# Token weights fetched and placed earlier, two squares moved from ScalarE to GpSimd, and one value cast moved later, in a fused attention and mixer kernel

## The chip, the cores and the metric

The kernel runs on one core of one Trainium2 chip. A core has a matrix engine (TensorE, PE in the profile; PEld is its loading of weights), VectorE (DVE), ScalarE (ACT), GpSimd (POOL), and SyncE (SP), which here only issues transfers. Each engine executes its own instructions in order; semaphores tie them together. The metric is the device time of one execution in microseconds (us); less is better. Three executions of the kernel before took 393.38, 394.13 and 394.23 us, median 394.13.

## What is computed

Cosine attention for 8 batches of 12 heads, sequence 448, head size 64, and behind it an MLP mixer over the tokens and then the channels:

```python
# q, k, v: (8, 12, 448, 64) fp32, tau = 0.1
q_n = q / (norm(q, axis=-1) + 1e-6)
k_n = k / (norm(k, axis=-1) + 1e-6)
scores = q_n @ k_n^T / tau
attn = softmax(scores)                        # exp and division by the row's sum
x = (attn @ v), heads side by side            # (8, 448, 768)
h = relu(x^T @ w_tok1) @ w_tok2               # (448, 256), (256, 448): over tokens
u = x + h^T
h2 = relu(u @ w_ch1) @ w_ch2                  # (768, 1536), (1536, 768): over channels
out = u + h2                                  # fp32
```

## The kernel before

The work goes by pairs of heads: 48 pairs, six per batch; three pairs make a "half" of a batch, the unit in which q, k and v are loaded. Of the 448 rows of a head, 384 lie as three rows on each of 128 partitions (the main part, tiles `qm`, `km`, `vm`); the last 64 are loaded apart (`xq`, `xk`, `xv`).

A pair goes through these steps:

- **Norms.** `squares` (L182) squares q and k of the pair into a tile `sq`, of which two exist; `squares_x` (L187) does the last 64 rows of a half's three pairs into one tile `sqx`. `square` (L176) runs on the engine that it is given; its instruction is L178 on ACT, L180 elsewhere. `sums` (L191) and `sums_x` (L196) add up per head and row on DVE (L193, L197), and `rnorms` (L199) makes inverse norms by four activations on ACT (L201 to L204).
- **Scaling.** `scaled` (L206) and `scaled_x` (L214) multiply k and q by the inverse norms into `kq` (L211, L217, L222), on POOL but for pair 0.
- **Transposes.** For the first 15 pairs, `tpose` (L253) turns `kq` around on PE (L243, L247, L248) into a PSUM tile, and `qk_copy` (L260) brings it to SBUF on DVE (L261).
- **Scores.** `score` (L295) multiplies k by q for a third of the main rows (PE, L301; two matmuls beside each other) and takes the exponential on ACT (L302); `score_x` (L305) does the last rows (L308, L309).
- **Values.** `cast_v` (L165) and `cast_vx` (L169) turn v of a half into fp16 (L166, on DVE for halves 0 to 2; L172, on POOL). `pv` (L311) multiplies by the exponentials (PE, L320, L322); a column of ones in the values gives the sums, and DVE takes reciprocals (L326) and multiplies (L327) to make `x`.
- **Token mixing.** `m_tok1` (L337) multiplies by `w1t` (L341) and DVE applies the relu into `r` (L344). `m_tok2` (L348) multiplies by `w2t` (L361), adds `x` by a matmul with the identity (L366) and DVE copies the result into `ut` (L368).
- **Channel mixing.** When a batch's six pairs are through, its units `m_ch1` (L389, relu on ACT at L391) and `m_ch2` (L404, DVE adds at L407, SP sends) go into a queue, and `feed` (L438) takes some from it in every slot.

PSUM has two small tiles (tag "b": transposes, U, the channel products) and three large ones (tag "s": scores, values, psR), so a product waits until the consumer of an earlier one has emptied its tile.

The order is written out by hand: everything under `tc.manual_schedule()` (L512) is issued in the program's order on each engine. First comes a prologue for pair 0 (L513 to L592); then a loop over `i`, here called slots (L593). Slot `i` computes the scores of pair `i`, the values of pair `i - 1`, and in the first slots the token mixing of earlier pairs. Tables say in which slot what is begun: `sq_at` for squares, `sum_at` for their sums, `rn_at` for inverse norms, `sc_at` for scaling, `cast_at` and `castx_at` for the casts, and so on (L455 to L481).

The token weights have a path of their own. `weights_tok` (L140) issues three transfers from POOL: the main rows of `w_tok1`, its last 64 rows, and `w_tok2` into a staging tile `w2n`. They are issued at the end of the prologue (L589). `place_w2` (L146) copies `w2n` in the order that the kernel's rows have into `w2t` on DVE: the main part (L147) and the last 64 columns behind it (L149); `place_w2_odd` (L151) writes the same 64 columns in front, for batches with an odd number (L152). `place_w2` comes at the end of slot 2, `place_w2_odd` at the end of slot 3. Pair 0's U needs `w2t` in slot 3.

In slot 0 the squares of pair 3 begin half 1: q and k of the pair, then xq and xk, all four on ACT. The cast of half 1's values is issued in slot 3 (`cast_at`), before the slot's U; pair 3's values are multiplied in slot 4.

SP issues the loads of q, k, v in the order of the prologue (L513 to L533), among them v of half 0 (L528), the rest of q and k of half 1 (L530, L531) and v of half 1 (L532); the loads for half 2 start in slot 0.

Of the kernel before, what the change touches and what calls it, by code (L numbers as in the profile page):

```python
# [16 lines left out]
def _bcast_free(ap: bass.AP, n: int) -> bass.AP:  # L17
    new_ap = list(ap.ap) + [[0, n]]
    return bass.AP(tensor=ap.tensor, offset=ap.offset, ap=new_ap)
# [3 lines left out]
def kernel(  # L23
# [12 lines left out]
    nc = tc.nc  # L36

    B, H, S, E = q.shape
# [5 lines left out]
    NC = 3  # L44
    SM = P * NC
    XR = S - SM
# [7 lines left out]
    NP_ALL = B * NPAIR  # L54
    HP = 3
    NHALF = 2 * B
# [19 lines left out]
    w1t = cst.tile([P, NC + 1, T], FP16, name="w1t")  # L76
    w2t = cst.tile([P, TT, XR + S], FP16, name="w2t")
# [12 lines left out]
    w2n = []  # L90
# [43 lines left out]
    def xh(at, n, w):  # L134
        return at[n // 2][:, w * (n % 2):w * (n % 2) + w]

    def mh(at, p):
        return at[p // HP][:, 2 * (p % HP):2 * (p % HP) + 2]

    def weights_tok():  # L140
        nc.gpsimd.dma_start(out=w1t[:, 0:NC, :], in_=moe_w_tok1[0:SM].rearrange("(p c) t -> p c t", c=NC))
        nc.gpsimd.dma_start(out=w1t[0:XR, NC, :], in_=moe_w_tok1[SM:S])
        w2n.append(mix.tile([P, TT, S], FP16, name="w2n", tag="gt16", bufs=1))
        nc.gpsimd.dma_start(out=w2n[0][:], in_=moe_w_tok2.rearrange("(tt p) s -> p tt s", p=P))

    def place_w2():  # L146
        nc.vector.tensor_copy(out=w2t[:, :, XR:S].rearrange("t a (c p) -> t a c p", c=NC),  # L147
                              in_=w2n[0][:, :, 0:SM].rearrange("t a (p c) -> t a c p", c=NC))
        nc.vector.tensor_copy(out=w2t[:, :, S:S + XR], in_=w2n[0][:, :, SM:S])  # L149

    def place_w2_odd():  # L151
        nc.vector.tensor_copy(out=w2t[:, :, 0:XR], in_=w2n[0][:, :, SM:S])  # L152

    def weights_ch1(i):
        n = C // 2
# [9 lines left out]
    def cast_v(n):  # L165
        (nc.vector if n < 3 else nc.gpsimd).tensor_copy(out=vts[n % NV][:, :, :, 0:E].rearrange("p g c e -> p (g c) e"),  # L166
                              in_=vm[n][:].rearrange("p g c e -> p (g c) e"))

    def cast_vx(n):  # L169
        for g in range(2):  # L170
            r = slice(XR * g, XR * (g + 1))
            nc.gpsimd.tensor_copy(out=vxs[n % NV][r, :, E1 * g:E1 * g + E], in_=xh(xv, n, HP)[r])  # L172
# [3 lines left out]
    def square(eng, out, src):  # L176
        if eng is nc.scalar:
            nc.scalar.activation(out=out, in_=src, func=AF.Square)  # L178
        else:
            eng.tensor_tensor(out=out, in0=src, in1=src, op=ALU.mult)  # L180

    def squares(p, eq, ek):  # L182
        sq[p] = nrm.tile([P, 2, 2 * NC, E], FP32, name=f"sq_{p}", tag="sq")
        for a, (eng, src) in enumerate(((eq, mh(qm, p)), (ek, mh(km, p)))):
            square(eng, sq[p][:, a], src.rearrange("p g c e -> p (g c) e"))

    def squares_x(n, eq, ek):  # L187
        square(eq, sqx[0:XR, 0:6], xh(xq, n, 6))
        square(ek, sqx[:, 6:9], xh(xk, n, HP))

    def sums(p, a0=0, a1=2):  # L191
        lo = 9 + 12 * (p % HP)
        nc.vector.tensor_reduce(out=ssqs[p // HP % 3][:, lo + 6 * a0:lo + 6 * a1],  # L193
                                in_=sq[p][:, a0:a1].rearrange("p a g e -> p (a g) e"), axis=AXX.X, op=ALU.add)

    def sums_x(n):  # L196
        nc.vector.tensor_reduce(out=ssqs[n % 3][:, 0:9], in_=sqx[:], axis=AXX.X, op=ALU.add)  # L197

    def rnorms(n, c0=0, c1=45):  # L199
        ssq, rn = ssqs[n % 3][:, c0:c1], rns[n % 3][:, c0:c1]  # L200
        nc.scalar.activation(out=rn, in_=ssq, func=AF.Ln, bias=tiny[:])  # L201
        nc.scalar.activation(out=rn, in_=rn, func=AF.Exp, scale=0.5)
        nc.scalar.activation(out=rn, in_=rn, func=AF.Ln, bias=eps[:])  # L203
        nc.scalar.activation(out=rn, in_=rn, func=AF.Exp, scale=-1.0)  # L204

    def scaled(p, eng):  # L206
        n, j = p // HP, p % HP
        for a, src in enumerate((mh(km, p), mh(qm, p))):
            lo = 9 + 12 * j + 6 * (1 - a)
            rn = rns[n % 3][:, lo:lo + 6].rearrange("p (g c) -> p g c", g=2)  # L210
            eng.tensor_tensor(out=kqs[n % 2][:, j, a, 0:NC, :].rearrange("p c (g e) -> p g c e", g=2),  # L211
                              in0=src, in1=_bcast_free(rn, E), op=ALU.mult)
# [28 lines left out]
    def tpose_main(p, pst, a):  # L241
        for c in range(NC):
            nc.tensor.transpose(pst[:, P * (4 * a + c):P * (4 * a + c + 1)], kqs[p // HP % 2][:, p % HP, a, c], id16[:])  # L243
# [61 lines left out]
    def score_x(p):  # L305
        qk, pt = qks[p], pts[p % 2]
        psX = ps2.tile([P, 2, 512], FP32, name=f"psX_{p}", tag="s")[:, 0, :]
        nc.tensor.matmul(psX[:, 0:S], qk[:, P * NC:P * (NC + 1)], qk[:, 512:512 + S], start=True, stop=True)  # L308
        nc.scalar.activation(out=pt[:, PX:PX + S], in_=psX[:, 0:S], func=AF.Exp, scale=inv_tau)  # L309
# [137 lines left out]
    def at(slots):  # L447
        got = {}
        for p, s in slots.items():
            got.setdefault(s, []).append(p)  # L450
        return got


    FIRST = NPAIR
    early_sq = {3: 0, 4: 1, 5: 1, 6: 3, 7: 4, 8: 5, 9: 5, 10: 6, 11: 7, 12: 8, 13: 9, 14: 9, 15: 10, 16: 11, 17: 11}  # L455
    sq_slot = {p: early_sq.get(p, p - 6) for p in range(3, NP_ALL)}
    sq_at = at(sq_slot)
    sum_at = at({p: s + 1 for p, s in sq_slot.items() if p < 8 or p >= 18})

    rn_at = {}  # L460
    for n in range(1, NHALF):
        for c0, c1 in ((0, 21), (21, 45)) if n < 4 else ((0, 45),):
            s = 1 + sq_slot[3 * n + (0 if c1 == 21 else 2)]
            rn_at.setdefault(s, []).append((n, c0, c1))
    sc_at = at({p: {7: 6}.get(p, p - 2 if p < DMA_FROM else p - 3) for p in range(3, NP_ALL)})
    early_qk = {2: 0, 3: 4, 4: 6, 5: 7}
# [3 lines left out]
    x_at = at({b: {1: 0, 2: 6, 3: 11}.get(b, 6 * b - 8) for b in range(1, B)})  # L470
    xq_at = at({b: {1: 0, 2: 6, 3: 11}.get(b, 6 * b - 9) for b in range(1, B)})
    xv_at = at({b: {1: 1, 2: 9}.get(b, 6 * b - 4) for b in range(1, B)})
    cast_at = at({n: {1: 3, 2: 6}.get(n, 3 * n - 2) for n in range(1, NHALF)})
    castx_at = at({n: {1: 2, 2: 6}.get(n, 3 * n - 2) for n in range(1, NHALF)})
    tok_slot = {p: FIRST if p in (FIRST - 2, FIRST - 1) else p + 2 for p in range(NP_ALL)}
    tok_at = at(tok_slot)
# [20 lines left out]
    def norm_begin(p, eq, ek):  # L497
        squares(p, eq, ek)
        if p % HP == 0:
            squares_x(p // HP, eq, ek)  # L500

    def norm_sums(p):
        sums(p)
        if p % HP == 0:
            sums_x(p // HP)
# [6 lines left out]
    with tc.manual_schedule():  # L512
# [53 lines left out]
        tpose_main(0, pst, 0)  # L566
        tpose_main(0, pst, 1)
        squares_x(0, nc.scalar, nc.gpsimd)
        rnorms(0, 21, 33)
        scaled(1, nc.gpsimd)  # L570
        nc.scalar.copy(out=qks[0][:, 0:SM], in_=pst[:, 0:SM])
# [14 lines left out]
        rnorms(0, 33, 45)  # L586
        score_rest0()
        score_x(0)
        weights_tok()  # L589
        cast_vx(0)  # L590
        cast_v(0)
        scaled(2, nc.gpsimd)  # L592
        for i in range(NP_ALL + 2):  # L593
            if i < DMA_FROM:
# [25 lines left out]
            def norm_rn():  # L620
                for n, c0, c1 in rn_at.get(i, ()):
                    rnorms(n, c0, c1)

            def next_sq(ps):
                for p in ps:
                    norm_begin(p, nc.scalar if p < 18 else nc.gpsimd, nc.scalar if p == 3 else nc.vector if p in (10, 11, 12, 15) else nc.gpsimd)

            if i == FIRST:
                next_sq([9])
                rnorms(2, 21, 33)  # L630
                norm_scale(7, nc.gpsimd)
                pv(i - 1)
                m_tok1(i - 2)
                tok2(i - 3)
                next_qk(i)
                tok2(i - 2)
                m_tok1(i - 1)
                score(i, 0)
                score(i, 1)
                score(i, 2)  # L640
                tok2(i - 1)
                norm_sums(8)
                norm_sums(9)
            elif 0 < i < NP_ALL:
                score(i, 0, 2 if i < 4 else 0)
                score(i, 1)
                score(i, 2)
            for p in sum_at.get(i, ()):
                norm_sums(p)
            if i < FIRST:  # L650
                norm_rn()

            if i < FIRST:
                next_sq([p for p in sq_at.get(i, ()) if p != 9])
                for p in sc_at.get(i, ()):
                    norm_scale(p, nc.gpsimd)
# [26 lines left out]
            elif i == FIRST:  # L683
# [5 lines left out]
                rnorms(3, 0, 21)  # L689
                next_qk(i + 1)  # L690
                next_sq(sq_at[i])
                norm_sums(10)
                feed(0.0, 1000.0)
# [34 lines left out]
                        norm_sums(p)  # L728
                feed(quota * 0.4, 900.0 if i >= 2 * NPAIR else 0.0)
            if i == 2:  # L730
                place_w2()
            if i == 3:
                place_w2_odd()
        for p in ut_at.get(NP_ALL + 2, ()):
            u_tpose(p)
        feed(1e9)
# [35 lines left out]
```

## Time and profile before

| | |
|---|---|
| median of three executions | 394.13 us |
| lowest and highest | 393.38, 394.23 us |
| the profiled execution, its time | 393.38 us |
| its span in the profile | 391.6 us |
| bytes moved, mean rate | 67.51 MB, 172 GB/s |
| mean granted TensorE clock | 0.991 |

The profile is of one execution. Times in it are in us from the start of the span. A row of the answers in order of time has the start, the duration, the engine, the line of the kernel and the operation, the tile written and the tiles read with their shapes, how many instructions were merged, and in brackets the idle time of the engine before it and what ended that. A row of the answers by stretches has the stretch, its length, the busy time of PE, PEld, DVE, ACT and POOL with the number of instructions, the granted TensorE clock as a share of full speed, the mean busy share of the 16 DMA engines (over 1 where packets overlap) and GB/s.

Stretches of the opening, in the same columns but without the counts:

| us | PE | PEld | DVE | ACT | POOL | clock | DMA | GB/s |
|---|---|---|---|---|---|---|---|---|
| 0 to 5 | 3.63 | 1.34 | 1.99 | 2.22 | 2.54 | 1.00 | 0.62 | 175 |
| 5 to 10 | 4.17 | 1.68 | 3.49 | 3.82 | 2.42 | 1.00 | 1.04 | 228 |
| 10 to 15 | 2.36 | 1.37 | 3.63 | 4.52 | 4.92 | 0.76 | 0.94 | 273 |
| 20 to 25 | 4.15 | 2.78 | 4.07 | 4.90 | 3.37 | 1.00 | 1.16 | 258 |
| 30 to 35 | 4.25 | 3.04 | 4.93 | 4.44 | 3.34 | 1.00 | 1.04 | 215 |
| 35 to 40 | 4.54 | 3.36 | 3.15 | 4.97 | 4.69 | 1.00 | 1.12 | 240 |
| 40 to 45 | 4.54 | 3.03 | 3.54 | 2.16 | 2.25 | 1.00 | 1.16 | 286 |
| 60 to 70 | 10.00 | 6.50 | 7.94 | 8.78 | 4.79 | 1.00 | 1.15 | 207 |

Transfers of the opening that the change concerns:

| transfer | issued at | KB | us to landing |
|---|---|---|---|
| v, half 0 | 8.18 | 576 | 5.0 |
| rest of q, half 1 | 10.13 | 384 | 5.9 |
| rest of k, half 1 | 10.77 | 384 | 6.5 |
| v, half 1 | 11.32 | 576 | 8.8 |
| w_tok1, main rows | 12.71 | 192 | 6.8 |
| w_tok1, last rows | 13.44 | 32 | 6.5 |
| w_tok2 | 14.35 | 224 | 7.2 |

### The profile page before, as it was taken

What the parts mean: (1) busy time and instruction counts of PE and PEld (TensorE: products, weight loads), DVE (VectorE), ACT (ScalarE), POOL (GpSimd) and SP (SyncE); (2) the same over time, 40 slices, a digit from 0 to 9 for tenths busy, and PEclk for the clock granted to TensorE, in tenths of its full rate; (3) what the DMA queues carried; (4) which work ended last, traced back from release to release, by engine and by line L of the source; (5) the groups of instructions that cost most, each with busy time, mean ns of one, the idle gap of its engine ahead of it and who ended that gap; (6) DMA issues with size and microseconds to landing.
All of it is one profiled execution on the core that took longest, in us unless ns stands there. A gap on an engine that the chain in (4) does not pass through costs nothing.

```text
span 391.6 us, 9075 instructions
## 1 busy us (share of the span) xinstructions
PE 378.7 (97%) x3658; PEld 228.9 (58%) x3658; DVE 193.6 (49%) x368; ACT 226.1 (58%) x411; POOL 209.6 (54%) x306
## 2 busy tenths in 40 slices
PE   7678999999999999999999999999999999999996
PEld 2356655665565656565566565565566566565554
DVE  5688758866244654446534545346434342333022
ACT  5998698843765548673775546673765535511400
POOL 4978486589476675768673938658551700000000
PEclk9699999999999999999999999999999999999999
DMA  8999989988988988999999899799982453023013
GB/s 204 267 242 221 256 238 187 201 213 241 208 170 200 211 166 194 222 166 223 199 239 174 177 253 206 155 192 175 244 142 55 133 114 69 16 60 102 3 40 121
DMA packets 137514, 67.51 MB, mean 172 GB/s; under 512 B 93248, under 2 KB 134016, under 8 KB 137472
## 3 DMA queue, kind: packets, MB, share of 16 engines
q1 hardware_dynamic: 133296, 61.36, 72.0%
q0 software_dynamic: 3632, 5.18, 7.7%
q8 instruction: 28, 0.46, 0.5%
q10 hardware_dynamic: 544, 0.39, 0.3%
q14 instruction: 14, 0.11, 0.1%
HBM read 43.38 MB, written 11.01 MB: 139 GB/s over the span
## 4 chain that ended last, share of the span: by engine, by line
PE 88%; ACT 7%; DVE 3%; DMA 1%; issue 1%; SPq 0%; DVEq 0%
PE psF L404 28%; PE psG L389 28%; PE psO L320 9%; PE psS L301 7%; PE psR L341 5%; PE psU L361 4%; ACT pt L302 3%; PE psO L322 3%; PE psX L308 2%; DMA qm<-in_q_dram 1%; PE psU L366 1%; ACT sq L178 1%; PE pst L243 1%; ACT pt L309 1%; ACT rn L203 1%
## 5 line engine op out<-in xcount | busy, mean ns | idle before, releaser
L302 ACT ACTIVATE pt<-psS 128x896 f16<-128x896 f32 x141 | 119.1, 921 | 64.6 <-PE psS L301 64.3
L389 PE MATMUL psG<-ut,wc1t 128*128 128x448 f16 x576 | 119.5, 353 | 0.2
L404 PE MATMUL psF<-wc2t,gt 128*128 128x384 f16 (+2 forms) x684 | 117.3, 323 | 0.1
L391 ACT ACTIVATE gt<-psG 128x448 f16<-128x448 f32 x96 | 51.1, 557 | 71.9 <-PE psG L389 71.9
L404 PEld LDWEIGHTS <-gt 128*128 128x128 f16 x684 | 64.5, 98 | 47.1 <-issue 6.8
L389 PEld LDWEIGHTS <-wc1t 128*128 128x128 f16 x576 | 53.2, 98 | 52.4 <-issue 8.7
L211 POOL TENSOR_TENSOR kq<-km,rn 128x384 f16<-128x384 f32 x47 | 39.4, 838 | 77.4 <-ACT rn L204 77.2
L407 DVE TENSOR_TENSOR ost<-psF,ur 128x384 f32<-128x384 f32 (+2 forms) x57 | 31.4, 550 | 87.2 <-PE psF L404 87.2
L320 PEld LDWEIGHTS <-pt 128*128 128x128 f16 x1152 | 50.8, 98 | 8.5 <-issue 2.4
L320 PE MATMUL psO<-vt,pt 128*128 128x65 f16 x1152 | 53.1, 194 | 1.1 <-ACT pt L302 0.8
L326 DVE RECIPROCAL rec<-psO 128x8 f32<-128x8 f32 x48 | 9.9, 207 | 81.5 <-PE psO L322 81.5
L193 DVE TENSOR_REDUCE ssq<-sq 128x12 f32<-128x768 f32 (+1 forms) x49 | 45.1, 929 | 6.0 <-ACT sq L178 3.1
L180 POOL TENSOR_TENSOR sq<-km 128x384 f32<-128x384 f32 x42 | 34.4, 822 | 15.1 <-DMA km<-in_k_dram 14.8
L322 PE MATMUL psO<-vx,pt 128*128 128x130 f16 x192 | 42.1, 219 | 0.0
L211 POOL TENSOR_TENSOR kq<-qm,rn 128x384 f16<-128x384 f32 x47 | 39.6, 842 | 0.0
L301 PE MATMUL psS<-qk 64*128 64x448 f16 x282 | 36.2, 357 | 1.3 <-DVE qk L261 0.9
L327 DVE TENSOR_TENSOR x<-psO,rec 128x512 f16<-128x512 f32 x48 | 33.2, 691 | 1.7
L341 PE MATMUL psR<-x,w1t 128*128 128x128 f16 x384 | 29.2, 219 | 0.1
L309 ACT ACTIVATE pt<-psX 128x448 f16<-128x448 f32 x48 | 27.1, 564 | 3.3 <-PE psX L308 2.3
L361 PE MATMUL psU<-w2t,r 128*128 128x448 f16 x96 | 25.9, 353 | 1.5 <-DVE w2t L149 1.1
L180 POOL TENSOR_TENSOR sq<-qm 128x384 f32<-128x384 f32 x30 | 24.7, 823 | 1.1 <-DVE ssq L193 0.3
L341 PEld LDWEIGHTS <-w1t 128*128 128x128 f16 x384 | 23.8, 97 | 2.1 <-issue 0.4
(76 smaller groups left out, 320.4 us busy)
## 6 DMA issues: line engine op xcount, KB each, us to landing
vm<-in_v_dram SPq DMA_DIRECT2D x16, 576.0 KB, 5.3
out_dram<-ost SPq DMA_DIRECT2D x23, 384.0 KB, 2.9
qm<-in_q_dram SPq DMA_DIRECT2D x14, 576.0 KB, 5.2
km<-in_k_dram SPq DMA_DIRECT2D x14, 576.0 KB, 5.2
wc1t<-in_moe_w_ch_dram POOLq DMA_DIRECT2D x2, 1152.0 KB, 13.9
wc2t<-in_moe_w_ch_dram POOLq DMA_DIRECT2D x2, 1152.0 KB, 12.9
out_dram<-ost SPq DMA_DIRECT2D x9, 192.0 KB, 2.7
xq<-in_q_dram SPq DMA_DIRECT2D x7, 192.0 KB, 5.1
```

Of the source, the lines that this page charges most:

```text
L180: eng.tensor_tensor(out=out, in0=src, in1=src, op=ALU.mult)
L193: nc.vector.tensor_reduce(out=ssqs[p // HP % 3][:, lo + 6 * a0:lo + 6 * a1], in_=sq[p][:, a0:a1].rearrange("p a g e -> p (a g) e"), axis=A ...
L211: eng.tensor_tensor(out=kqs[n % 2][:, j, a, 0:NC, :].rearrange("p c (g e) -> p g c e", g=2), in0=src, in1=_bcast_free(rn, E), op=ALU.mult)
L301: nc.tensor.matmul(psS[:, g, 0:S], qk[r, P * c:P * (c + 1)], qk[r, 512:512 + S], start=True, stop=True)
L302: nc.scalar.activation(out=pt[:, 2 * S * c:2 * S * (c + 1)].rearrange("p (g s) -> p g s", g=2), in_=psS[:, :, 0:S], func=AF.Exp, scale=inv ...
L320: nc.tensor.matmul(psO[:, m, E1 * g:E1 * (g + 1)], pt[:, at:at + P], vt[:, 2 * j + g, c, 0:E1], start=(g == 0 and c == 0), stop=False)
L322: nc.tensor.matmul(psO[:, m, 0:2 * E1], pt[:, PX + P * m:PX + P * (m + 1)], vx[:, j, 0:2 * E1], start=False, stop=True)
L341: nc.tensor.matmul(psR[:, tt, :], w1t[:, m, tt * P:(tt + 1) * P], xs[p][:, m, :], start=(m == 0), stop=(m == NC))
L361: nc.tensor.matmul(psU, rs[p][:, tt, :], w2t[:, tt, lo:lo + S], start=(tt == 0), stop=by_dma and tt == TT - 1)
L389: nc.tensor.matmul(psG[:], wc1t[:, dt, ct * P:(ct + 1) * P], ut[:, dt, sp], start=(dt == 0), stop=(dt == DT - 1))
L391: nc.scalar.activation(out=gt[:, ct, sp], in_=psG[:], func=AF.Relu)
L404: nc.tensor.matmul(psF[:, 0:w], gt[:, ct, lo:lo + P], wc2t[:, ct, P * i0:P * i1], start=(ct == 0), stop=(ct == CT - 1))
```

## The change

- The transfer of `w_tok2` and that of the main rows of `w_tok1` are issued from POOL ahead of pair 1's scaling (after the prologue's `squares_x(0, ...)`); the last rows of `w_tok1` stay where all three were.
- The main part of `w2t` is placed in slot 1, after that slot's sums, instead of at the end of slot 2. The two copies of the last 64 columns stay at the ends of slots 2 and 3.
- The squares of half 1's last rows and of pair 3 move from slot 0 to the end of the prologue, before the scaling of pair 2; those of `xk` and of pair 3's k are made by POOL instead of ACT, and ACT squares xq before pair 3's q.
- The cast of half 1's values moves from before slot 3's U to the end of slot 3.
- The tables lose the entries for pair 3's squares and half 1's cast. The slots of the sums and inverse norms stay.

The words that name the change also speak of three output tiles; the pool of output tiles has three buffers in both kernels (L69).

```diff
-    def weights_tok():
-        nc.gpsimd.dma_start(out=w1t[:, 0:NC, :], in_=moe_w_tok1[0:SM].rearrange("(p c) t -> p c t", c=NC))
-        nc.gpsimd.dma_start(out=w1t[0:XR, NC, :], in_=moe_w_tok1[SM:S])
+    def weights_tok1(x):
+        if x:
+            nc.gpsimd.dma_start(out=w1t[0:XR, NC, :], in_=moe_w_tok1[SM:S])
+        else:
+            nc.gpsimd.dma_start(out=w1t[:, 0:NC, :], in_=moe_w_tok1[0:SM].rearrange("(p c) t -> p c t", c=NC))
+
+    def weights_tok2():
         w2n.append(mix.tile([P, TT, S], FP16, name="w2n", tag="gt16", bufs=1))
         nc.gpsimd.dma_start(out=w2n[0][:], in_=moe_w_tok2.rearrange("(tt p) s -> p tt s", p=P))
 
     def place_w2():
         nc.vector.tensor_copy(out=w2t[:, :, XR:S].rearrange("t a (c p) -> t a c p", c=NC),
                               in_=w2n[0][:, :, 0:SM].rearrange("t a (p c) -> t a c p", c=NC))
-        nc.vector.tensor_copy(out=w2t[:, :, S:S + XR], in_=w2n[0][:, :, SM:S])
-
-    def place_w2_odd():
-        nc.vector.tensor_copy(out=w2t[:, :, 0:XR], in_=w2n[0][:, :, SM:S])
+
+    def place_w2_x(lo):
+        nc.vector.tensor_copy(out=w2t[:, :, lo:lo + XR], in_=w2n[0][:, :, SM:S])
...
-    early_sq = {3: 0, 4: 1, 5: 1, 6: 3, 7: 4, 8: 5, 9: 5, 10: 6, 11: 7, 12: 8, 13: 9, 14: 9, 15: 10, 16: 11, 17: 11}
-    sq_slot = {p: early_sq.get(p, p - 6) for p in range(3, NP_ALL)}
+    early_sq = {4: 1, 5: 1, 6: 3, 7: 4, 8: 5, 9: 5, 10: 6, 11: 7, 12: 8, 13: 9, 14: 9, 15: 10, 16: 11, 17: 11}
+    sq_slot = {p: early_sq.get(p, p - 6) for p in range(4, NP_ALL)}
...
-    cast_at = at({n: {1: 3, 2: 6}.get(n, 3 * n - 2) for n in range(1, NHALF)})
+    cast_at = at({n: {2: 6}.get(n, 3 * n - 2) for n in range(2, NHALF)})
...
         squares_x(0, nc.scalar, nc.gpsimd)
+        weights_tok2()
+        weights_tok1(0)
         rnorms(0, 21, 33)
         scaled(1, nc.gpsimd)
...
         score_x(0)
-        weights_tok()
+        weights_tok1(1)
         cast_vx(0)
         cast_v(0)
+        squares_x(1, nc.scalar, nc.gpsimd)
+        squares(3, nc.scalar, nc.gpsimd)
         scaled(2, nc.gpsimd)
...
-                    norm_begin(p, nc.scalar if p < 18 else nc.gpsimd, nc.scalar if p == 3 else nc.vector if p in (10, 11, 12, 15) else nc.gpsimd)
+                    norm_begin(p, nc.scalar if p < 18 else nc.gpsimd, nc.vector if p in (10, 11, 12, 15) else nc.gpsimd)
...
             for p in sum_at.get(i, ()):
                 norm_sums(p)
+            if i == 1:
+                place_w2()
             if i < FIRST:
                 norm_rn()
...
             if i == 2:
-                place_w2()
+                place_w2_x(S)
             if i == 3:
-                place_w2_odd()
+                place_w2_x(0)
+                cast_v(1)
```

More of the change, by code (lines that the diff above doesn't have):

```diff
@@ L454 @@
     FIRST = NPAIR
-    early_sq = {3: 0, 4: 1, 5: 1, 6: 3, 7: 4, 8: 5, 9: 5, 10: 6, 11: 7, 12: 8, 13: 9, 14: 9, 15: 10, 16: 11, 17: 11}
-    sq_slot = {p: early_sq.get(p, p - 6) for p in range(3, NP_ALL)}
+    early_sq = {4: 1, 5: 1, 6: 3, 7: 4, 8: 5, 9: 5, 10: 6, 11: 7, 12: 8, 13: 9, 14: 9, 15: 10, 16: 11, 17: 11}
+    sq_slot = {p: early_sq.get(p, p - 6) for p in range(4, NP_ALL)}
     sq_at = at(sq_slot)
-    sum_at = at({p: s + 1 for p, s in sq_slot.items() if p < 8 or p >= 18})
+    sum_at = at({p: s + 1 for p, s in ({3: 0} | sq_slot).items() if p < 8 or p >= 18})
     rn_at = {}
@@ L462 @@
         for c0, c1 in ((0, 21), (21, 45)) if n < 4 else ((0, 45),):
-            s = 1 + sq_slot[3 * n + (0 if c1 == 21 else 2)]
+            s = 1 + ({3: 0} | sq_slot)[3 * n + (0 if c1 == 21 else 2)]
             rn_at.setdefault(s, []).append((n, c0, c1))
```

## The prediction

> **What bounds the kernel now.** I read the page's shares and chain first, then stretches of the span, then the order in time on each engine between 12 and 39 us, where all the edited instructions run.
>
> The head of the page, and then two answers on stretches (the columns after the stretch are its length and the busy time of PE, PE's weight loads, DVE, ACT and POOL, then the granted clock, the DMA share and GB/s):
>
> ```profile
> span 391.6 us, 9075 instructions
> PE 378.7 (97%) x3658; PEld 228.9 (58%) x3658; DVE 193.6 (49%) x368; ACT 226.1 (58%) x411; POOL 209.6 (54%) x306
> PE 88%; ACT 7%; DVE 3%; DMA 1%; issue 1%; SPq 0%; DVEq 0%
> ```
> ```profile
> 15.00:20.00 5.00, 4.73 (x47) 2.67 (x45) 2.53 (x5) 4.93 (x11) 3.95 (x7) 0.56 1.17 271
> 25.00:30.00 5.00, 3.86 (x56) 2.45 (x54) 4.58 (x8) 3.99 (x8) 4.47 (x6) 1.00 1.04 216
> 100.00:150.00 50.00, 50.00 (x526) 30.83 (x523) 24.10 (x45) 30.37 (x52) 31.09 (x44) 1.00 0.94 195
> ```
>
> TensorE has no gap after the opening, so whatever the opening gains or loses reaches the end one for one, and nothing later can gain. The opening is bound in turn by ACT (15 to 20), DVE (25 to 35) and TensorE. In 15 to 20 TensorE ran at 0.56 of its clock.
>
> PE in order of time, with what ended its idle time in brackets:
>
> ```profile
> 16.28 1.30 PE L301 MATMUL psS<-qk 64*128 64x448 f16 x6
> 25.41 0.89 PE L301 MATMUL psS<-qk 64*128 64x448 f16 x6
> 27.44 0.54 PE L361 MATMUL psU<-w2t,r 128*128 128x448 f16 x2 [1.14 <-DVE w2t L149]
> 35.01 1.03 PE L301 MATMUL psS<-qk 64*128 64x448 f16 x6 [0.57 <-DVE qk L261]
> ```
>
> and DVE, POOL and ACT around it:
>
> ```profile
> 25.56 1.09 DVE L147 COPY w2t<-w2n 128x768 f16<-128x768 f16 x1
> 26.57 0.81 DVE L149 COPY w2t<-w2n 128x128 f16<-128x128 f16 x1
> 27.31 0.93 DVE L166 CAST vt<-vm 128x1152 f16<-128x1152 f32 x1
> 31.00 0.49 DVE L152 COPY w2t<-w2n 128x128 f16<-128x128 f16 x1
> 31.41 0.94 DVE L193 TENSOR_REDUCE ssq<-sq 128x12 f32<-128x768 f32 x1
> ...
> 25.40 0.83 POOL L211 TENSOR_TENSOR kq<-km,rn 128x384 f16<-128x384 f32 x1 [1.41 <-ACT rn L204]
> 26.19 1.14 POOL L211 TENSOR_TENSOR kq<-qm,rn 128x384 f16<-128x384 f32 x1
> 30.62 0.82 POOL L211 TENSOR_TENSOR kq<-km,rn 128x384 f16<-128x384 f32 x1
> ...
> 16.52 0.36 ACT L178 ACTIVATE sqx<-xk 128x192 f32<-128x192 f32 x1
> 16.88 2.54 ACT L302 ACTIVATE pt<-psS 128x896 f16<-128x896 f32 x3
> ```
>
> Two things matter. PE stands 1.14 us because the two w2 copies end at 27.39. And DVE and POOL take turns: L149 ends at 27.39, 0.05 after POOL's product ends (27.34), and L152, the same size, ends at 31.50, 0.06 after POOL's (31.44); the POOL product that ran beside L147 and L149 took 1.14 instead of 0.82. [...]
>
> **The change part by part** (slot i is pass i of the loop).
>
> *ACT loses two squares in slot 0.* 15.69 to 16.10 and 16.52 to 16.88 go: 0.77 us. But the exponentials of slot 1 (16.88) also wait for their scores, written 16.28 to 16.84 at half clock. ACT is then ready 0.65 early and waits. Taken: 0. Ends: 0, and -0.65 if those scores came that much earlier. The half clock is seen from 12 to 20 us of this execution (granted 0.80, then 0.50, 0.79 at the end). [...]
>
> *Two of three token fetches move ahead of pair 1's products on POOL.* An issue takes 0.73 and 0.74 us; POOL is idle from 7.47 to 8.91, 1.45 us. Taken 0; the third issue took 0.92 beside DVE work, so up to +0.2, which pair 1's transpose (14.27, its products end 10.53) and the sums of pair 2 (12.40, POOL's square ends 11.31) both cover.
>
> *Their bytes move too.* 224 + 192 KB now go out with the first V and the rest of q and k of half 1, not with the second V. SP's queue keeps its order; all that is behind gets later. From 14 to 17 us the DMA moved 318 to 347 GB/s, from 17 to 19, with the weights in flight, 213 to 217. So 416 KB cost 1.3 us at the first rate, and 1.0 more if 3 us run at the second: 1.3 to 2.3. The w1 fetch issued at 12.71 showed in the rate at about 17, 4 us later; so the weights start near 11.4, when the first V (issued 8.18, landed 5.0 later, 13.2) is half through. It lands 0.6 to 2.3 later, 13.8 to 15.5. Waiting behind it on DVE: cast_v(0) (13.50, 0.75), then pair 1's qk copy (15.42, ends 16.08), and then PE's scores (16.28). The cast must end by 15.65, so V must land by 14.85. Taken: 0 (the middle, 14.6). Ends: 0 and +0.65.
>
> *POOL takes the squares of xk and of pair 3's k.* 0.50 + 0.82 = 1.32 us before pair 2's products (15.97), against 1.47 taken off in front of them. POOL also waits for xv (cast_vx), late by the same DMA: at worst about 15.8, so products end near 19.4; pair 2 is transposed at 19.69. Taken 0. The sums of pair 3 on DVE (16.26) now wait for POOL instead of ACT: 15.5 to 17.8.
>
> *Main part of w2 in slot 1.* 1.09 us (L147) into DVE's idle time from 17.87 to 19.70, 1.83 us. Taken 0. With the sums at 17.8 it no longer fits: up to +0.6 on the reciprocal at 19.70.
>
> *Slot 2 keeps only the 128-element copy.* It asks at 25.56, after POOL's product of 25.40; ends 0.05 after that one (26.24), 26.29. PE's scores end at 26.30; U starts at 26.35 instead of 27.44: **-1.09**. The cast of V half 1 is gone from here too, so U's copy is not held. Pair 4's q product now ends near 26.98, before PE's transposes need it (27.09). V products of pair 2, psX, and DVE's reciprocal (29.82 to 28.74) follow at -1.09. ACT's part of slot 3 follows at -0.99 (its squares end 29.15).
>
> *Slot 4: DVE is the chain.* From 29.82 to the qk copy of pair 5 (34.30 to 34.95) DVE never stops, and PE's scores at 35.01 wait for it. That chain starts 1.09 earlier, and gets cast_v(1) in it. POOL is earlier too: no 1.14 product, no held casts, so its fetch of w_ch1, squares and pair 5's products move from 30.62 to about 29.83. DVE asks for the odd w2 copy at 31.00 - 1.09 = 29.92, behind POOL's product (until 30.65): ends 30.70, 0.79 instead of 0.49, **+0.30**. Then POOL's second product, already waiting, goes first, as it did at 26.65 between L147 and L149: until 31.45; the cast then needs 0.62 (27.62 to 28.24 behind POOL's cast): next instruction at 31.98 instead of 30.62, **+1.36**. [...]
>
> Sum: 0 + 0 - 1.09 + 0.30 + 1.36 = **+0.57 us**, ends -0.70 (port never held) and, with +0.65 from the late V, +1.22; the 0.6 of the w2 copy adds at most part. Behind slot 4 the shift goes on: exponentials of pair 5 (35.41), psX (38.23), V product at 38.84 waiting for that, then PE. w_ch1's first half (landing 42.4, wanted 44.54) and the late k of half 3 (42.75, its sums at 45.28) stay covered.
>
> The profiled execution took 393.38 us, 391.6 span and 1.8 around it; it is the fastest of three, whose median is 394.13. So 393.95 on its own, 394.70 on the median.
>
> **The rivals.**
>
> *Slower: the weights get in front of V.* One mechanism: 416 KB between the SP queue's packets, from the landing of V at 14.85 on. For it: the DMA share is 0.88 or more from 11 us, the rate fell by a third with these weights, and DVE executes in order, so a late cast stops pair 1's copy. Against: half of V is through by then. At 15.5: +0.65, plus some 0.2 of the 0.6 where the w2 copy now meets the reciprocal, plus the +0.57 of the sum: +1.4, **395.5**.
>
> [...]
>
> [...]
>
> **How the numbers follow.** A measurement of this kernel can tell about 0.2%, 0.79 us, from no change. Forecast, +0.57 with the moved wait in it: 0.42 (0.32 of it inside 0.79, 0.10 slower). Late V: 0.28 (0.26 slower, 0.02 inside). Free port: 0.30 (0.24 faster, 0.06 inside). So 0.24 faster, 0.40 no change, 0.36 slower. The range runs from 392.9, where the free port with part of ACT's time ends, to 395.8, a little above the late V with the full 0.6.
>
> **What would show it.** Right: no PE wait on w2t before U, U near 26.4; cast_v(1) over 1 us long near 30.6 to 32; PE's slot 5 scores waiting for the qk copy at about 35.5; exponentials of slot 1 still at 16.9. Late V: cast_v(0) waiting for DMA beyond 14.85 and slot 1's scores after 16.4. Free port: odd copy under 0.2 us, slot 5's scores before 34.5. Wrong altogether: a shift that arises after 45 us, where I expect none, or another half-clock stretch.

## The result, and the profile after

The changed kernel took 396.00 us (median of five, 395.96 to 396.1), the kernel before beside it 393.92: a ratio of 1.0054 [1.0039, 1.0069]. Repeated later, it took 395.54 beside 393.51, 1.0051 [1.0038, 1.0063]. It is some 2.0 us slower. The forecast was +0.57, and its range ended at 395.8.

The head of the page of the kernel after, and three answers on stretches:

```profile
span 394.2 us, 9074 instructions
PE 378.1 (96%) x3658; PEld 229.1 (58%) x3658; DVE 194.6 (49%) x368; ACT 225.4 (57%) x409; POOL 210.4 (53%) x308
PE 88%; DVE 4%; DMA 3%; ACT 3%; SPq 1%; issue 1%; POOL 0%; ACTq 0%; POOLq 0%; DVEq 0%
```
```profile
20.00:25.00 5.00, 2.83 (x41) 1.75 (x40) 4.07 (x6) 4.42 (x11) 4.92 (x7) 0.95 1.17 237
25.00:30.00 5.00, 5.00 (x43) 3.03 (x40) 2.72 (x6) 3.25 (x8) 3.36 (x7) 0.71 1.10 211
100.00:150.00 50.00, 49.85 (x501) 30.01 (x501) 24.11 (x45) 30.30 (x50) 32.05 (x45) 1.00 0.90 189
```

The busy time is within 1 us of the one before on every engine; in the chain that ended last ACT's share fell from 7% to 3% and DMA's rose from 1% to 3%, 2% of it the load of `xv`. TensorE is still full at 100 to 150 (busy 49.85 of 50 us), so the loss lies in the opening. In 20 to 25 TensorE was busy for 2.83 us, against 4.15 before. In 25 to 30 it ran at 0.71 of its clock: this execution had a second half-clock stretch there (24.51 to 27.92).

PE of the kernel after, in order of time:

```profile
16.93 1.10 PE L304 MATMUL psS<-qk 64*128 64x448 f16 x6
22.44 0.74 PE L304 MATMUL psS<-qk 64*128 64x448 f16 x6 [1.54 <-DVE qk L264]
28.80 0.55 PE L364 MATMUL psU<-w2t,r 128*128 128x448 f16 x2
37.59 0.74 PE L304 MATMUL psS<-qk 64*128 64x448 f16 x6 [1.03 <-DVE qk L264]
```

and DVE and POOL:

```profile
10.50 2.03 DVE L220 TENSOR_TENSOR kq<-xq,rn 64x128 f16<-64x128 f32 x1 [0.67 <-ACT rn L207]
...
15.46 0.76 DVE L169 CAST vt<-vm 128x1152 f16<-128x1152 f32 x1 [1.23 <-DMA vm<-in_v_dram]
16.14 0.65 DVE L264 COPY qk<-pst 128x960 f16<-128x960 f16 x1
18.24 0.95 DVE L196 TENSOR_REDUCE ssq<-sq 128x12 f32<-128x768 f32 x1 [1.45 <-POOL sq L183]
19.11 0.74 DVE L200 TENSOR_REDUCE ssq<-sqx 128x9 f32<-128x576 f32 x1
19.77 1.21 DVE L151 COPY w2t<-w2n 128x768 f16<-128x768 f16 x1
20.90 0.19 DVE L329 RECIPROCAL rec<-psO 128x8 f32<-128x8 f32 x1
```
```profile
7.57 0.89 POOL L148 DMA_DIRECT2D w2n<-in_moe_w_tok_dram  x1
8.46 0.58 POOL L144 DMA_DIRECT2D w1t<-in_moe_w_tok_dram  x1
...
9.85 0.83 POOL L214 TENSOR_TENSOR kq<-qm,rn 128x384 f16<-128x384 f32 x1
10.64 0.82 POOL L183 TENSOR_TENSOR sq<-km 128x384 f32<-128x384 f32 x1
11.42 0.60 POOL L220 TENSOR_TENSOR kq<-xq,rn 64x256 f16<-64x256 f32 x1
```

A row starts when its engine comes to the instruction, called asking here; its duration is read here as holding any wait for the other engine, since the same 64x128 product took 0.28 us in e8, where POOL only issued a transfer, 0.89 before and 2.03 here. What the lines show: the wait of U for `w2t` (1.14 before) is gone. But pair 1's scores start at 16.93 instead of 16.28, those of pair 2 stand 1.54 for DVE (0.35 before), and those of pair 5 stand 1.03 for it (0.57 before). Ahead of each lies DVE work that came late or took long: a product of 2.03 us that took 0.89 before, a cast that waited for V until 15.44 (V landed at 13.14 before), the w2 copy that ends at 20.98 while the V products for the reciprocal behind it end at 19.64, and, ahead of pair 5, the moved cast, 1.43 us long (shown under e9).

The starts of a slot's first exponentials measure this step by step. The second profile of the changed kernel (e9 below) had only one half-clock stretch, of the same length as before, and is the fair partner of the profile before:

| step, us | before | after, first profile | after, second profile | difference, second |
|---|---|---|---|---|
| start of slot 1 | 16.88 | 17.53 | 17.55 | +0.67 |
| slot 1 to 2 | 4.79 | 5.32 | 5.19 | +0.40 |
| slot 2 to 3 | 4.14 | 5.68 | 4.14 | 0.00 |
| slot 3 to 4 | 5.20 | 4.21 | 4.22 | -0.98 |
| slot 4 to 5 | 4.40 | 5.26 | 6.00 | +1.60 |
| slot 5 to 6 | 7.98 | 7.98 | 7.98 | 0.00 |
| sum | | | | +1.69 |

The spans differ by 393.3 - 391.6 = 1.7 (these two executions took 395.06 and 393.38), so the steps account for all of it. In the first profile the sum is 2.59, of 2.6: there the second stretch of half clock added 1.54 in slot 2, and slot 4 cost 0.74 less.

### The profile page after: what moved, and what is told of

Same layout as the page of the kernel before. It is cut to its first block, busy times and chain, and to the rows that moved or that the text cites. A ratio compares the mean times of both kernels' runs of the same rounds, so it can differ in the third digit from the quotient of the medians.

```text
span 394.2 us, 9074 instructions
## 1 busy us (share of the span) xinstructions
PE 378.1 (96%) x3658; PEld 229.1 (58%) x3658; DVE 194.6 (49%) x368; ACT 225.4 (57%) x409; POOL 210.4 (53%) x308
## 4 chain that ended last, share of the span: by engine, by line
PE 88%; DVE 4%; DMA 3%; ACT 3%; SPq 1%; issue 1%; POOL 0%; ACTq 0%; POOLq 0%; DVEq 0%
PE psF L407 28%; PE psG L392 27%; PE psO L323 9%; PE psS L304 7%; PE psR L344 5%; PE psU L364 4%; PE psO L325 3%; PE psX L311 2%; DMA xv<-in_v_dram 2%; ACT pt L305 1%; DMA km<-in_k_dram 1%; PE pst L246 1%; PE psU L369 1%; DVE x L330 1%; DVE ssq L196 0%
## 5 line engine op out<-in xcount | busy, mean ns | idle before, releaser
L183 POOL TENSOR_TENSOR sq<-km 128x384 f32<-128x384 f32 x43 | 35.6, 830 | 11.7 <-DMA km<-in_k_dram 11.5
L304 PE MATMUL psS<-qk 64*128 64x448 f16 x282 | 35.4, 355 | 3.2 <-DVE qk L264 2.6
```

What stands on the lines that cost most here:

```text
L304: nc.tensor.matmul(psS[:, g, 0:S], qk[r, P * c:P * (c + 1)], qk[r, 512:512 + S], start=True, stop=True)
```

## The experiments

All were timed in five rounds beside the kernel before (393.65, 393.80 and 393.51 us in the three groups). The intervals of the ratios come to 0.4 to 0.7 us each way.

**e1: the early fetches alone.** The two transfers of `weights_tok2` and `weights_tok1(0)` ahead of pair 1's scaling, all else as before.

```diff
         squares_x(0, nc.scalar, nc.gpsimd)
+        weights_tok2()
+        weights_tok1(0)
...
-        weights_tok()
+        weights_tok1(1)
```

> The kernel before with the early token fetches alone. Port theory: POOL's products start 0.1 us later and run without a gap, DVE's first scaled_x product (0.89 us before, 2.03 in the changed kernel) loses its turn again, and slot 1's exponentials start near 17.5 instead of 16.9: +0.65 us. DMA theory: the products keep 0.9 us, the cast of V waits until 15.4 and delays slot 1 by 0.1 to 0.3 us only. Clock theory (a second half-clock stretch comes from TensorE's idle time): no second stretch here, since DVE's w2 copy does not stand before slot 1's reciprocal; were it to come from the fetches, +1.5 more.

394.58 us, 1.0024 [1.0014, 1.0034]: +0.9. DVE of e1:

```profile
10.64 1.93 DVE L221 TENSOR_TENSOR kq<-xq,rn 64x128 f16<-64x128 f32 x1 [0.67 <-ACT rn L208]
...
15.51 0.76 DVE L170 CAST vt<-vm 128x1152 f16<-128x1152 f32 x1 [1.25 <-DMA vm<-in_v_dram]
16.18 0.65 DVE L265 COPY qk<-pst 128x960 f16<-128x960 f16 x1
```

Both delays of the kernel after are here, the long product and the late V. The exponentials of slot 1 start at 17.56 (+0.68), and the later steps are as before (4.87, 4.14, 5.21, 4.41). So the first term of the table is the early fetches' doing. Which of the two delays does it, this run can't say: both release pair 1's copy at the same time, 16.1 to 16.2. e5 and e6 below part them.

**e8: early issues without the bytes.** Two more fetches of the 32 KB piece at the same place, into a tile that is loaded again later.

```diff
         squares_x(0, nc.scalar, nc.gpsimd)
+        for _ in range(2):
+            nc.gpsimd.dma_start(out=w1t[0:XR, NC, :], in_=moe_w_tok1[SM:S])
```

> The kernel before with two extra issues of the 32 KB fetch at the place of the early fetches; the real fetches stay late, so POOL's time is taken but 416 KB are not moved ahead of V. Port theory: as e1, +0.65 us. DMA theory: V lands at 13.2 as before, 0 us.

395.42 us, 1.0043 [1.0031, 1.0055]. The experiment was not clean: the second issue waited 2.29 us for the first to land, and POOL's products began at 11.05 instead of 8.91. V landed at 13.39, so the price here is not V's. The run does show one thing, in these lines of DVE and POOL:

```profile
10.80 3.69 DVE L222 TENSOR_TENSOR kq<-xk,rn 64x64 f16<-64x64 f32 x2
```
```profile
11.05 0.84 POOL L211 TENSOR_TENSOR kq<-km,rn 128x384 f16<-128x384 f32 x1
11.85 0.83 POOL L211 TENSOR_TENSOR kq<-qm,rn 128x384 f16<-128x384 f32 x1
12.63 0.82 POOL L180 TENSOR_TENSOR sq<-km 128x384 f32<-128x384 f32 x1
13.42 0.60 POOL L217 TENSOR_TENSOR kq<-xq,rn 64x256 f16<-64x256 f32 x1
```

The first of these two small DVE products (3.34 us of the 3.69; 0.63 before) asked at 10.80, before any of these POOL instructions began, and ended at 14.14, after all four of them.

**e11: one fetch early.** Only `w_tok2` (224 KB) goes ahead of pair 1's scaling; both pieces of `w_tok1` stay.

```diff
         squares_x(0, nc.scalar, nc.gpsimd)
+        weights_tok2()
```

> The kernel before with the fetch of w_tok2 alone ahead of pair 1's products (0.9 us in 1.45 us of POOL's idle time), the two of w_tok1 late as before. Port theory (POOL's products start 0.1 us later and DVE asks during the q product instead of the square): here they start on time, DVE's first scaled_x product takes 0.89 us, the V of half 0 lands some 1 us late, and slot 1's exponentials stay at 16.9 to 17.0: 0 to +0.2 us in all. DMA theory (the bytes in front of V make the +0.9 us of the two early fetches): half of it, +0.4 us, with the product at 0.89 us.

393.72 us, 1.0004 [0.9995, 1.0013]: no price clear of the interval. DVE of e11:

```profile
10.95 0.90 DVE L219 TENSOR_TENSOR kq<-xq,rn 64x128 f16<-64x128 f32 x1 [0.67 <-ACT rn L206]
...
14.60 0.76 DVE L168 CAST vt<-vm 128x1152 f16<-128x1152 f32 x1 [0.62 <-DMA vm<-in_v_dram]
15.81 0.66 DVE L263 COPY qk<-pst 128x960 f16<-128x960 f16 x1 [0.45 <-PE pst L250]
```

POOL's q product ended at 10.92, before DVE asked, and the product took its 0.90. V landed at 14.58, 1.4 later than before, and pair 1's copy still waited for PE and not for the cast. Neither delay is on the path, so this run too leaves open which one matters. The +0.4 that the DMA theory gave it lies inside the interval of the time, but the rows show nothing of it (the distances under e6).

**e5: the w2 main part back at the end of slot 2**, all else as after. It was made for the price of `place_w2` in slot 1.

```diff
-            if i == 1:
-                place_w2()
...
             if i == 2:
+                place_w2()
                 place_w2_x(S)
```

> The changed kernel with the main part of w2 placed at the end of slot 2 again. If the 1.21 us copy in front of slot 1's reciprocal makes slot 2 late and through it the second half-clock stretch: the reciprocal comes 0.5 to 1.2 us earlier, TensorE stands less, the clock stays full, and although U waits some 1 us for w2 again, the time falls by 1 us or more against the changed kernel (395 or less). Rival (the placement costs nothing, the fetch and the cast cost all): slower than the changed kernel by the 1 us wait, 397.

395.63 us, 1.0052 [1.0035, 1.0070], the same as the kernel after within the interval, where the gain and the price of the move in the table differ by about half a microsecond: not decided by the times. Its profile had a half clock from 12.66 to 22.9, so its step from slot 1 to 2 can't be used; slot 3 took 5.19 again, so the gain of 0.98 there does come from the w2 copies. Neither of the expected times came (395 or less, or 397). By chance it also separates the two delays of e1. DVE and PE of e5:

```profile
10.45 0.90 DVE L220 TENSOR_TENSOR kq<-xq,rn 64x128 f16<-64x128 f32 x1 [0.67 <-ACT rn L207]
...
15.89 0.76 DVE L169 CAST vt<-vm 128x1152 f16<-128x1152 f32 x1 [2.40 <-DMA vm<-in_v_dram]
16.56 0.65 DVE L264 COPY qk<-pst 128x960 f16<-128x960 f16 x1
```
```profile
17.27 1.30 PE L304 MATMUL psS<-qk 64*128 64x448 f16 x6 [1.02 <-DVE qk L264]
```

With both fetches early, POOL's q product happened to end at 10.42 here, before DVE asked at 10.45: no long product. V landed at 15.86, the cast waited 2.40 us for it, and pair 1's scores stood 1.02 us. The late V is enough by itself, where it comes this late. In the kernel after, where pair 1's transposes also ended late, at 16.0 instead of 15.4, the long product hides it.

**e2: the cast moved alone.** The cast of half 1 at the end of slot 3, all else as before.

```diff
-    cast_at = at({n: {1: 3, 2: 6}.get(n, 3 * n - 2) for n in range(1, NHALF)})
+    cast_at = at({n: {2: 6}.get(n, 3 * n - 2) for n in range(2, NHALF)})
...
                 place_w2_odd()
+                cast_v(1)
```

> The kernel before with the cast of V's half 1 alone moved to the end of slot 3. The chain on DVE in slot 4 gets the cast in it: +0.7 us with the port free, up to +1.6 held, and the wait for w2 stays. Rival: DVE's slot 3 gets as much earlier as slot 4 gets later, 0.

395.35 us, 1.0044 [1.0032, 1.0056]: +1.7. **e6** is the opposite, the changed kernel with the cast back before slot 3's U:

```diff
-    cast_at = at({n: {2: 6}.get(n, 3 * n - 2) for n in range(2, NHALF)})
+    cast_at = at({n: {1: 3, 2: 6}.get(n, 3 * n - 2) for n in range(1, NHALF)})
...
                 place_w2_x(0)
-                cast_v(1)
```

> The changed kernel with the cast of V's half 1 back before slot 3's U. The cast took 1.43 us in slot 4's chain on DVE; without it some 1.2 us come off (394.8). Rival: the cast then stands before U's copy and takes 0.9 back, 395.7.

394.33 us, 1.0013 [1.0002, 1.0023]: 0.5 above the kernel before, and by the ratios (1.0054 and 1.0051) 1.5 to 1.6 below the changed kernel. DVE of e2, then of e6:

```profile
30.82 0.85 DVE L152 COPY w2t<-w2n 128x128 f16<-128x128 f16 x1
31.59 1.43 DVE L166 CAST vt<-vm 128x1152 f16<-128x1152 f32 x1
```
```profile
27.09 0.75 DVE L169 CAST vt<-vm 128x1152 f16<-128x1152 f32 x1
```

and POOL of e6 beside it:

```profile
27.07 1.44 POOL L214 TENSOR_TENSOR kq<-qm,rn 128x384 f16<-128x384 f32 x1
```

In e2 the step from slot 4 to 5 grew from 4.40 to 6.12, and no other step changed by more than 0.13. The cast that took 1.43 there takes 0.75 in e6, and not because POOL is away: POOL's product beside it takes 1.44 instead of 0.82. One of the two waits, and in slot 4 it is DVE, on the path. Measured alone, the moved cast is the largest cost of the change. In e6's profile slot 4 takes 4.78 instead of 6.00, but slot 3 takes 4.71 instead of 4.22, since the cast is back in it. By these two steps the late cast costs 0.73 in the changed kernel, by the times 1.5 to 1.6; why they differ is open.

e6 also has the long product with V not in the way:

```profile
10.69 1.99 DVE L220 TENSOR_TENSOR kq<-xq,rn 64x128 f16<-64x128 f32 x1 [0.67 <-ACT rn L207]
...
15.10 0.76 DVE L169 CAST vt<-vm 128x1152 f16<-128x1152 f32 x1 [0.72 <-DMA vm<-in_v_dram]
16.21 0.66 DVE L264 COPY qk<-pst 128x960 f16<-128x960 f16 x1 [0.35 <-PE pst L251]
```

The cast was over at 15.86, and pair 1's copy waited for the transposes alone. The exponentials of slot 1 begin 6.99 us after DVE asked for its 64x128 product. That distance is 6.31 or 6.32 in the five profiles with neither delay and the half clock over pair 1's transposes (before, e2, e7, e11, e12), 7.41 in e5, and 6.90 to 7.14 with both delays (the changed kernel, e1, e4, e9, e10). So the long product alone costs 0.68, and beside it the late V adds 0.15 at most.

**e3: the squares alone.** Half 1's last rows and pair 3 squared in the prologue, two of the squares by POOL.

```diff
         cast_v(0)
+        squares_x(1, nc.scalar, nc.gpsimd)
+        squares(3, nc.scalar, nc.gpsimd)
         scaled(2, nc.gpsimd)
```

> The kernel before with the squares of pair 3's k and of half 1's xk made by POOL and half 1's squares issued in the prologue, nothing else. ACT is ready earlier, but slot 1's exponentials wait for half-clock scores: no gain. POOL's products of pair 2 end near 18.8 instead of 17.6 and the sums of pair 3 start near 17.2: 0 to +0.3 us. Rival: the late POOL delays slot 2, +1 us.

393.19 us, 0.9986 [0.9977, 0.9995]: a gain of 0.55, where 0 to +0.3 was expected. Among runs of equal mean clock it is 0.45 (0.991) and 0.42 (0.996). Here the exponentials of slot 1 began at 16.20. ACT of e3:

```profile
15.35 0.52 ACT L178 ACTIVATE sqx<-xq 64x384 f32<-64x384 f32 x1
15.76 0.51 ACT L178 ACTIVATE sq<-qm 128x384 f32<-128x384 f32 x1
16.20 2.54 ACT L302 ACTIVATE pt<-psS 128x896 f16<-128x896 f32 x3
```

ACT goes over without a wait, 0.68 earlier than before. In this execution the half clock began at 14.85 instead of 12.59, pair 1's transposes ran at full clock, and the scores began at 15.61, so they did not hold ACT. In the changed kernel ACT waits 0.68 us for them.

**e4 and e10: more filling matmuls in slot 2** (products whose result is not used), against the second half-clock stretch of the first profile: nine, then five, where the changed kernel has two.

```diff
-                score(i, 0, 2 if i < 4 else 0)
+                score(i, 0, 9 if i == 2 else 2 if i < 4 else 0)
```

> The changed kernel with seven more filling matmuls ahead of slot 2's scores, in the 1.54 us in which TensorE stands there. Clock theory: the granted clock stays full from 24 to 28 us and the time falls by about 1.5 us against the changed kernel (396.0 to 394.5, +0.6 against before). Rival (the step from slot 2 to 3 is late because of DVE or POOL): unchanged, or worse by the filling, 396 or more.

> The changed kernel with three more filling matmuls ahead of slot 2's scores instead of the seven tried first, so that they end before the scores may start even at half clock. Clock theory: no second stretch, and runs up to 1.5 us shorter than the unedited kernel on the same chip. Rival (the stretch hardly counts over the runs): same as the unedited kernel.

**e9: the changed kernel again**, beside e10.

> The changed kernel once more, unedited, for a second profile and the granted clock of each run. If the second half-clock stretch (24.5 to 27.9 us) is part of the change's cost, most runs show a mean clock near 0.990 and the profile has it again. If it belongs to one execution, the runs with 0.991 or 0.996 are up to 1.5 us shorter, and the change costs about 1.0 to 1.7 us in them (port turn +0.65, w2 copy ahead of the reciprocal +0.5, slots 3 and 4 between -0.1 and +0.6).

e4: 395.91, 1.0055 [1.0042, 1.0068]. e10: 395.76, 1.0060 [1.0048, 1.0073]. e9: 395.54, 1.0051. No second stretch is in any of the three profiles, e9's included, which has no added filling, and the times are equal within their intervals. So the second stretch belongs to some executions, and filling does not help; e4's nine matmuls ran until the scores of slot 2 at 23.55, where e10's began at 22.34. The clock has a small part all the same: of the changed kernel's ten runs five had a mean granted clock of 0.987, of the 63 runs of the kernel before in these groups none. At an equal clock of 0.991 e9's three runs average 395.43 and the eleven of the kernel before beside them 393.67, so 1.76 us of the 2.0 are there without it. The lines of e9 for slot 4, DVE and then POOL:

```profile
30.99 0.85 DVE L155 COPY w2t<-w2n 128x128 f16<-128x128 f16 x1
31.76 1.43 DVE L169 CAST vt<-vm 128x1152 f16<-128x1152 f32 x1
33.11 0.94 DVE L196 TENSOR_REDUCE ssq<-sq 128x12 f32<-128x768 f32 x1
```
```profile
30.96 0.82 POOL L214 TENSOR_TENSOR kq<-km,rn 128x384 f16<-128x384 f32 x1
31.75 0.82 POOL L214 TENSOR_TENSOR kq<-qm,rn 128x384 f16<-128x384 f32 x1
```

The copy asks 0.03 behind POOL's product and ends 0.06 after it (31.84 and 31.78); the cast is behind the second product (until 32.57) and ends 0.62 after that. This is the prediction's slot 4.

**e7: another place for w2.** The kernel before, with `w_tok2` first of the three late fetches and its main part placed after slot 2's sums.

```diff
     def weights_tok():
+        w2n.append(mix.tile([P, TT, S], FP16, name="w2n", tag="gt16", bufs=1))
+        nc.gpsimd.dma_start(out=w2n[0][:], in_=moe_w_tok2.rearrange("(tt p) s -> p tt s", p=P))
         nc.gpsimd.dma_start(out=w1t[:, 0:NC, :], in_=moe_w_tok1[0:SM].rearrange("(p c) t -> p c t", c=NC))
...
+            if i == 2:
+                place_w2()
...
             if i == 2:
-                place_w2()
+                place_w2_x(S)
```

> The kernel before with w_tok2 fetched first of the three, still late, and the main part of w2 placed after slot 2's sums, in DVE's idle time from 22.9 to 23.8, the 128-element copy at the end of slot 2; cast and squares as before. If the 1.14 us wait is worth what the prediction says: U near 26.4, and since the cast ends before U's copy, -0.8 to -1.0 us (392.9 to 393.1). If POOL's last products of pair 3 are held by the copy (they end 23.99, PE wants them at 24.14), 0.3 to 0.4 of it are lost.

393.59 us, 0.9996 [0.9986, 1.0006]: no difference to be told. U starts at 26.56 instead of 27.44, and the main copy takes 0.55 there instead of 1.09; the POOL products beside it take 1.48 instead of 1.08, the loss that was expected as possible. The 0.74 that slot 3 gains is given back: 0.27 in slot 2 and 0.36 in slot 4, where the odd copy now takes 0.85.

**e12: what paid, put together.** e7 with e3's squares, and the odd copy at the end of slot 5, away from POOL's products.

```diff
             if i == 2:
                 place_w2_x(S)
-            if i == 3:
+            if i == 5:
                 place_w2_x(0)
```

> A version meant to beat both: the kernel before with POOL's squares (-0.55 us measured alone), w_tok2 fetched first but late and its main part placed after slot 2's sums (-0.2 measured alone, where the odd copy took 0.85 us in slot 4's chain on DVE), and the odd copy moved to the end of slot 5, out of that chain (0.41 us from start to start before, more when held). If the three add: -0.55 - 0.2 - 0.4 to -0.8 = -1.2 to -1.5 us, 392.2 to 392.6. Rival (ACT is the next bound in slot 4: the exponentials, inverse norms and squares there leave no gap): -0.7.

392.52 us, 0.9975 [0.9965, 0.9985]: 1.0 below the kernel before and 3.0 below the changed one beside it. The sum of 1.2 to 1.5 did not come, and part of the 1.0 is the clock: at equal mean clock the gain is 0.7 (0.996) and 0.8 (0.991, two runs). DVE of e12:

```profile
38.43 0.18 DVE L151 COPY w2t<-w2n 128x128 f16<-128x128 f16 x1
```

The odd copy takes 0.18. The cast of half 1, still before slot 3's U, met POOL's product there and took 1.43 as well, but the step from slot 3 to 4 is 4.22, as in the changed kernel, where the cast is not in it, and the next is 4.33: it cost nothing on the path.

## Why the prediction was wrong

The terms that the forecast added up, for slots 3 and 4, measured -0.98 + 1.60 = +0.62 in the second profile, against +0.57. What failed are terms that it put at nothing: they measured +0.67 ahead of slot 1 and +0.40 in slot 1.

The fetches, the cast and the squares measured alone sum to 0.9 + 1.7 - 0.55 = +2.05, and the change measured +2.0 and +2.1. That these agree is partly luck: the w2 placement is not in the sum, and ACT's gain is not found in the changed kernel's steps. What the w2 placement gains and costs is read from the step table.

- **Slot 3, -1.09:** right; -0.98. U no longer waits for `w2t`. It starts at 27.41 in the second profile, which is the 26.35 of the prediction plus the 1.07 that was lost ahead of it.
- **Slot 4, +0.30 and +1.36:** right; +1.60 to +1.74 in five of the six profiles with the late cast, and the time of e2 gives +1.7 (e6 above is less clear). In the sixth, the first of the changed kernel, it was +0.86, with an odd copy of 0.35. The late cast took 1.43 in all six. The -0.70 on record ("port never held"), on which the low end of the range and the chance of 0.30 rest, has both engines running at once in slot 4: an odd copy of some 0.13, which was my estimate and which no run shows, and 0.67 for the cast, from rows of 0.75 (13.50 and 47.66 before). The odd copy took 0.35 and 0.85 in the two profiles of the changed kernel, and 0.18 in e12, away from POOL's products.
- **"Taken 0; ... up to +0.2, which ... both cover", the fetch issues on POOL:** wrong, and the first step that failed. By the prediction's own rows two issues, 0.73 and 0.74 us, did not quite fit into the 1.45 us of idle time. And I counted the time that POOL had idle, not whom its later products would meet. The two issues (1.48 us in the run) moved POOL's q product of pair 1 from an end at 10.53, 0.04 before DVE asks for its own product, to 10.68, after it asks (10.50). DVE then lost its turn to the square and the next product, 2.03 us instead of 0.89. The transposes and the sums of pair 2 that I named as cover are what this delays, by some 0.6 (14.27 to 14.91, and 12.40 to 13.05), since both stand behind that product. e6 shows the price, 0.68.
- **"Taken: 0 (the middle, 14.6). Ends: 0 and +0.65", the bytes in front of V:** wrong by taking the middle. V landed at 15.44, nearly at the late end of 13.8 to 15.5. That rival's mechanism was there, as e5 shows. The two delays run side by side, so together they cost +0.67, once; e5 and e6, each with one of them, show that mending one alone would leave most of it.
- **"Taken 0 ... up to +0.6", the main w2 copy in slot 1:** wrong, +0.40 to +0.53 in the two profiles of the changed kernel. Pair 3's sums waited for POOL's squares until 18.24, later than the 17.8 that I had as the worst case, since POOL's squares stand behind `cast_vx`, which waited for xv until 15.7. The copy then ended at 20.98, beside POOL's squares 1.21 instead of 1.09. It is not a fixed price: in e6 the same copy ended at 20.62, the V products, at half clock up to 20.42, only at 20.55, and the step is 4.87, as in e1 without the copy.
- **ACT's two squares, taken 0:** right for this kernel, where the late scores eat the 0.65; e3 measures 0.55 for it alone. Its profile is of an execution whose scores were early; whether ACT's time counts with the scores at half clock is not shown.

The ends on record, all added, come near the result: 0.57 + 0.65 + 0.6 = 1.82, against 1.69 in the steps. The mistake was to treat the late V as an alternative and the w2 copy as counting "at most part". Both come from the transfers moved ahead of V and xv, and so they came together; that the 0.65 fits is partly luck, since the long product would have cost it without V. What the medians show above that (2.0 against 1.69) is partly the clock: 1.76 at an equal clock. The half-clock stretch that the prediction named as a way to be wrong appeared in one profile, but not as the main cause.

Open: each of the two prices ahead of slot 1 rests on one profile, e6 for the long product and e5 for the late V. The price of the w2 copy in slot 1 is shown in the steps of two profiles, not in times, and e6 has none. What the late cast costs in the changed kernel lies between the steps and the times of e6.

## What to carry to other kernels

Filling an idle gap of an engine shifts what stands behind it on that engine: here POOL's q product ended 0.15 us later, and one DVE product took 1.14 longer. Check which instruction of another engine each shifted one will now meet, above all where the two stand a tenth of a microsecond apart (0.04 here). And when several costs are "covered" by margins that one early transfer uses up together, add them rather than choose among them.

## What the runs showed of the hardware

A delay of 0.1 to 0.2 us on POOL cost DVE 1.0 to 1.1. In the seven profiles where DVE asked for its 64x128 product 0.03 to 0.04 us after POOL's q product had ended (before, e2, e3, e5, e7, e11, e12), it took 0.89 or 0.90; in the six where that product still ran for 0.06 to 0.18 (after, e1, e4, e6, e9, e10), 1.91 to 2.03, and there was nothing between. In e8, with POOL only issuing a transfer, it took 0.28. A DVE product that waits was passed by POOL instructions that began after it had asked: two at least in the changed kernel (10.64 and 11.42), four in e8. Which engine waits can change between kernels at the same place: for the cast of half 1 and the POOL product of the same moment the durations are 0.75 and 1.44 in e6, 0.75 and 1.45 in e7, but 1.43 and 0.83 in e12.

In the opening the half clock came in stretches of 3.4, 6.8 and 10.2 us (e3: 14.85 to 18.26; before: 12.59 to 19.42; e5: 12.66 to 22.9), and its start differed between two executions of one kernel: 14.27 in the first profile of the changed kernel, with a second stretch 10 us later, and 12.98 in the second.
